# The end of an attention and gated-FFN kernel: the last unit's value blocks in one PSUM bank, its heads in one operand, the last chunks shared evenly

## The chip, the core and the metric

The kernel runs on one core of a Trainium2 chip. Its engines run side by side, each in its own instruction order: PE (matrix products; PEld is its weight loading), DVE (vector operations), ACT (activations), POOL (general elementwise work), and SP, which here issues all transfers. Products are written to PSUM, eight banks of 128 partitions by 512 float32; the other memory on the core is SBUF. The metric is the device time of one execution in microseconds (us), lower is better.

## What is computed

```
xn  = layernorm(x)                          # x: 2048 x 512
q, k, v = split(xn @ wqkv), 32 heads of 16
o   = softmax(q k^T / 4) v                  # per head, 2048 x 2048 scores
s   = o @ wo                                # 512 x 512
y   = silu(((xn @ wg) * (xn @ wu)) @ wd)    # 1792 hidden columns
out = x + s * y
```

All is float32. Products of the projections and the FFN are split into hi and lo parts (a number rounded to the PE's fast float32 form, and the rest), and take three terms: hi x hi, hi x lo, lo x hi.

## The kernel before

**Units and blocks.** Attention runs over 32 units: a group of four heads times a chunk of 512 query rows, the chunk being the inner index. Unit 31 is thus the last group on the last chunk. A unit has 16 rounds, one for each 128 keys. A round has four positions, one for each head: a product `t` of keys and queries (L632) and its exponential on ACT (L634), and, until these run out, a score product and its maximum on DVE for a later unit. The main loop's block covers two rounds, eight positions, and then calls `values`, which issues `block` (L645): 16 products of exponentials with value columns, written to the four 32-partition quarters of one bank, `pv`. Each quarter holds a head's 16 output rows and a row with the sum of exponentials, in 32 rows. Positions run four ahead of the values.

**Banks.** Three banks have the tag "st", in turn for `t` and `pv`; three have the tag "s", for score products; two have the tag "misc", for the filler. A new tile waits until the one that held its bank before has been read.

**What becomes of pv.** The first block of a unit is copied to a sum in SBUF by ACT. Later ones are copied by ACT to `part` and added by POOL, or, in the last 21 rounds (`now[0] > NU * NT - LEAD // 4`), added straight from the bank by DVE (L653). When a unit is complete, `finish` transposes the sum on DVE in 32x32 blocks, divides by the sums of exponentials, transposes back, and stores the heads in the memory tensor `OD` of its chunk.

**The filler.** The `t` and `pv` products are interleaved with other PE work that a generator hands out, so many steps after each position: the projections, the FFN, and last `ending`. Most of this work comes as `pair`: two output tiles, each the sum of products with 64 contraction rows, one on the lower and one on the upper half of the array at a time. A pair has two halves of n steps; between them ACT reads one element of a bank (`look`, L294). `Filler.cycles` says over how many blocks a pair is spread, and `spread` shares the steps of a block out between its positions.

**The ending.** For each of the four chunks of 512 rows, o @ wo is made in two pairs of row tiles, z (L286, L290), 24 steps a pair. Chunks 0, 1 and 2 use complete heads: `o_split` loads the heads back from `OD` and splits them into hi and lo (`split_rows`, on POOL); `prepare` calls it as soon as a chunk's last unit is stored and buffers are there, and `until` lets a chunk begin three rounds behind that. `end` multiplies z by the stored silu(y) on DVE (L477), adds x on POOL, and stores the rows. Chunk 3 is split: `open_pair` makes the sum over heads 0 to 27, leaves the banks open, and the last four heads are added by `final`. Order of the pairs: chunk 0 (two), chunk 1 (two), the first open pair, chunk 2 (two), the second open pair. Their spread over blocks is the list `parts`, which `Filler.cycles` returns: 3 means three blocks, 2 two, 1 one.

**The tail.** The second half of the last open pair runs behind the last `pv`. Meanwhile `last_heads` takes unit 31's sum, in two halves of 256 columns: add the last pv (L692), transpose (L693), reciprocal, multiply (L695), transpose back (L696), then hi on ACT (L697) and lo on POOL. `final` multiplies each tile's columns with `wrh` and `wrl`, the hi and lo of the last four heads' rows of wo, laid at 16 of each 32 partitions, the others zero: hi x wrh, hi x wrl, lo x wrh (L554). Then `end` for the four last tiles, tile 1 all on DVE (L472, L473), tile 3 in two halves, tiles 0 and 2 with their add on POOL, and the stores.

PE, ACT, DVE and POOL keep the program's order; the order of SP's transfers is the scheduler's.

Of the kernel before, what the change touches and what calls it, by code (L numbers as in the profile page):

```python
# [11 lines left out]
F32 = mybir.dt.float32  # L12
F32R = mybir.dt.float32r
AF = mybir.ActivationFunctionType
OP = mybir.AluOpType
# [4 lines left out]
P = 128  # L20
S, D, H, DH, FF = 2048, 512, 32, 16, 1792
NT = S // P
NC = S // 512
# [8 lines left out]
LEAD = 86  # L32
# [16 lines left out]
def body(ctx, tc, x, wqkv, wo, wg, wu, wd, out):  # L49
    nc = tc.nc  # L50
# [3 lines left out]
    class Tied:  # L54

        on = True
# [14 lines left out]
    pool, sync = Tied(nc.gpsimd), Tied(nc.sync)  # L71
# [4 lines left out]
    def dmar(dst, src):  # L76
        sync.dma_start(dst.bitcast(F32), src.bitcast(F32))

    dram = ctx.enter_context(tc.tile_pool(name="dram", bufs=1, space=DRAM))
    keep = ctx.enter_context(tc.tile_pool(name="keep", bufs=1))  # L80
# [29 lines left out]
    fst = {}  # L110
# [6 lines left out]
    def psum(tag, name):  # L117
        ps, bufs = fst["ps"]
        return ps.tile([P, 512], F32, tag=tag, name=name, bufs=bufs[tag])
# [3 lines left out]
    def soon(n, fn):  # L123

        if n:
            waiting.append((steps[0] + n, fn))
            waiting.sort(key=lambda w: w[0])
        else:
            fn()
# [10 lines left out]
    before_values, behind_values = [], []  # L140
# [93 lines left out]
            return nc.vector.tensor_scalar(xt, xt, e[:, t:t + 1], mr[:, t:t + 1], op0=OP.mult, op1=OP.add)  # L234
        return nc.scalar.activation(xt, xt, AF.Identity, bias=mr[:, t:t + 1], scale=e[:, t:t + 1])

    def split_rows(raw, hi, lo):
        pool.tensor_copy(hi, raw)
        pool.tensor_tensor(lo, raw, hi, op=OP.subtract)

    def ln_turn(tt):
        c, t = divmod(tt, 4)
# [196 lines left out]
    def o_split(c, tiles):  # L439

        for d, (oh, ol) in enumerate(tiles):
            heads = 8 if c < NC - 1 or d < ND - 1 else 4
            n = heads * DH
            raw = (wtile(("w1r", "w0r")[d]).rearrange("p d q -> p (d q)") if d < 2 else
                   fst["fp"].tile([P, D], F32, name="wdr", bufs=2))
            dma(raw[:n], OD[c][8 * d:8 * d + heads, 0:DH])
            soon(4 + 5 * d // 2, lambda raw=raw[:n], oh=oh[:n], ol=ol[:n]: split_rows(raw, oh, ol))
        ops[c] = now[0], tiles

    def small_tiles():  # L450
# [15 lines left out]

    def end(c, t, o, yt, xt):
        tt = 4 * c + t
        if t % 2 and c == NC - 1:
            for h in range(1 if t == 1 else 2):  # L470
                part = slice(None) if t == 1 else slice(256 * h, 256 * h + 256)
                nc.vector.tensor_tensor(o[:, part], o[:, part], yt[:, part], op=OP.mult)  # L472
                nc.vector.tensor_tensor(yt[:, part], o[:, part], xt[:, part], op=OP.add)  # L473
                dma(out[tt * P:(tt + 1) * P, part], yt[:, part])
            return
        else:
            nc.vector.tensor_tensor(yt, o, yt, op=OP.mult)  # L477
            if c < NC - 1:
                behind_values.append(lambda: add(tt, yt, xt))
                return  # L480
            pool.tensor_tensor(yt, yt, xt, op=OP.add)
        dma(out[tt * P:(tt + 1) * P], yt)

    def add(tt, yt, xt):
        pool.tensor_tensor(yt, yt, xt, op=OP.add)
        dma(out[tt * P:(tt + 1) * P], yt)

    def o_terms(c, t):
# [5 lines left out]
    def ending():  # L494


        fp = fst["fp"]

        def big(n):
            return fp.tile([P, 5, 512], F32R, name=n)  # L500

        side = [big(n).bitcast(F32) for n in ("hh", "dl")]
        fst["big", 1] = big("hl"), big("dh")

        def until(c):
            while c not in ops or now[0] < ops[c][0] + SPLIT_ROUNDS:
                yield

        def chunk(c):
            yield from until(c)  # L510
            for t in range(0, 4, 2):
                here = side[t // 2]
                got = [(here[:, n], here[:, 2 + n]) for n in range(2)]

                def loads(t=t, here=here):
                    dma(here[:, 0:2], YD[c][:, t:t + 2])
                    dma(here[:, 2:4], x[(4 * c + t) * P:(4 * c + t + 2) * P].rearrange("(t p) d -> p t d", p=P))
                soon(2, loads)
                outs = []
                yield from pair(outs, [("misc", f"z{c}_{u}") for u in (t, t + 1)], [o_terms(c, u) for u in (t, t + 1)])  # L520
                for n, o in enumerate(outs):
                    before_values.append(lambda u=t + n, o=o, got=got[n]: end(c, u, o, *got))

        banks = []

        def open_pair(t, tag):
            outs = []
            ts = [o_terms(NC - 1, u) for u in (t, t + 1)]
            yield from pair(outs, [(tag, f"z{NC - 1}_{u}") for u in (t, t + 1)],
                            [a[:-3] for a in ts], [a[-3:] for a in ts], stop=False)  # L530
            banks.extend(outs)

        yield from chunk(0)
        fst["first"] = True
        yield from chunk(1)
        fst["big", 2] = big("hl"), big("dh")
        wr = fp.tile([P, D], F32, name="e2", bufs=1)
        pool.memset(wr, 0.0)
        for j in range(4):
            dma(wr[32 * j:32 * j + DH], wo[(H - 4 + j) * DH:(H - 3 + j) * DH])  # L540
        wrh, wrl = [t[:, 4] for t in fst["big", 2]]
        pool.tensor_copy(wrh, wr)
        pool.tensor_tensor(wrl, wr, wrh, op=OP.subtract)
        yield from until(NC - 1)
        yield from open_pair(0, "s")
        yield from chunk(2)
        xr = side[0][:, :4]
        dma(xr, x[(NC - 1) * 512:].rearrange("(t p) d -> p t d", p=P))

        def final(todo, kinds):  # L550
            for n in kinds:
                k, r = ((0, wrh), (0, wrl), (1, wrh))[n]
                for t in todo:
                    nc.tensor.matmul(banks[t], fst["t"][k][:, t * P:(t + 1) * P], r, start=False, stop=n == 2,  # L554
                                     skip_group_check=True)
            if 2 in kinds:
                for t in todo:
                    end(NC - 1, t, banks[t], fst["y"][:, t], xr[:, t])

        yield from open_pair(2, "misc")  # L560
        while "t" not in fst:
            yield
        for todo in (0, 1), (2, 3):
            final(todo, (0, 1))
            final(todo, (2,))

    NU = NG * NC
    QS, MX = {}, {}
    sums = {}
# [67 lines left out]
    def block(todo):  # L637

        i = todo[0][0]
        g = i // NC  # L640
        o = psum("st", f"pv{i}")
        for n, (_, kt, es) in enumerate(todo):
            for j in range(4):
                h0 = (4 * g + j) * VW
                nc.tensor.matmul(o[32 * j:32 * j + 32], V[:, kt, h0:h0 + 32], es[j],  # L645
                                 start=n == 0, stop=n == len(todo) - 1)
        if todo[-1][1] == NT - 1 and i == NU - 1:
            last_heads(o)
        elif todo[0][1] == 0:
            sums[i] = keep.tile([P, 512], F32, name="acc", bufs=2)  # L650
            nc.scalar.activation(sums[i], o, AF.Copy)
        elif now[0] > NU * NT - LEAD // 4:
            nc.vector.tensor_tensor(sums[i], o, sums[i], op=OP.add)  # L653
        else:
            part = part_tile()
            nc.scalar.activation(part, o, AF.Copy)  # L656
            pool.tensor_tensor(sums[i], sums[i], part, op=OP.add)
# [23 lines left out]

    def last_heads(o):

        i = NU - 1
        acc = sums.pop(i)
        tr = keep.tile([P, 16, 32], F32, name="tr", bufs=1)
        rc = keep.tile([P, 16, 1], F32, name="rc", bufs=1)
        th, tl = fst["t"] = [fst["fp"].tile([P, 512], F32, name="g", bufs=2).bitcast(F32R) for _ in range(2)]
        for h in range(2):
            c, b = slice(256 * h, 256 * h + 256), slice(8 * h, 8 * h + 8)  # L690
            flat = tr[:, b].rearrange("p b e -> p (b e)")
            nc.vector.tensor_tensor(acc[:, c], o[:, c], acc[:, c], op=OP.add)  # L692
            nc.vector.transpose(flat, acc[:, c])  # L693
            nc.vector.reciprocal(rc[:, b], tr[:, b, DH:DH + 1])
            nc.vector.tensor_tensor(tr[:, b, 0:DH], tr[:, b, 0:DH], rc[:, b].to_broadcast([P, 8, DH]), op=OP.mult)  # L695
            nc.vector.transpose(acc[:, c], flat)  # L696
            nc.scalar.activation(th[:, c], acc[:, c], AF.Copy)  # L697
            pool.tensor_tensor(tl[:, c], acc[:, c], th[:, c], op=OP.subtract)


    def run(gen):
# [130 lines left out]
    now = [0]  # L832
# [107 lines left out]
    with tc.manual_schedule(engines=ORDERED):  # L940
# [4 lines left out]
        q = 0  # L945
        for b in range(NU * NT // 2):
            if fil.done:
                parts = iter([3, 2, 3, 2, 2, 2, 1, 2])
                fil = Filler(ending(), lambda n: next(parts))
            work = fil.begin()  # L950
            if b >= NU * NT // 2 - 2:
# [50 lines left out]
```

## Time and profile before

| | us |
|---|---|
| median of 3 runs | 1711.33 (1711.22 to 1714.48) |
| the profiled execution | 1711.65 |
| its span in the trace | 1709.9 |
| mean granted PE clock of the span | 0.999 |
| last score maxima on DVE | about 1628 us into the span |
| last pv starts | 1695.76 us into the span |

Times in the trace are in us from the start of the span. "1663.49 1.92 PE L645 MATMUL pv<-e,V ... x16" is a group of 16 products that began at 1663.49 and ended 1.92 later; in brackets stands how long the engine was idle before, and what released it. In a row of stretches the first number is the length, then follow for each engine its busy time and, in brackets, its instructions, the granted clock, the share of the transfer engines, and GB/s.

### The profile page before, as it was taken

The page shows a single profiled execution, that of the slowest core. Times are in us where ns is not written, and L with a number is a line of the kernel's source. Part 1 is how long each engine was busy: PE and PEld are TensorE (multiplying, and loading weights), DVE is VectorE, ACT ScalarE, POOL GpSimd, SP SyncE. Part 2 cuts the span into 40 slices and gives each one's busy share as a digit, 9 for nine tenths or more (in the row PEclk, how much of TensorE's full clock was granted, in tenths as well). Part 3 has the DMA queues.
Part 4 walks back from the last instruction along what each step waited for, and adds up shares of the span by engine and source line. Part 5 has one row for each costly group of instructions (what it writes and reads, how often), then busy time and mean ns, then how long its engine had stood idle before and what let it go on. Part 6 is the DMA issues. An engine that isn't in the chain of part 4 may idle for free. (4 is left out here: it accounts for less than half of the span.)

```text
span 1709.9 us, 35015 instructions
## 1 busy us (share of the span) xinstructions
PE 1700.0 (99%) x13574; PEld 1043.2 (61%) x13574; DVE 1430.8 (84%) x2479; ACT 1308.5 (77%) x2568; POOL 888.2 (52%) x889
## 2 busy tenths in 40 slices
PE   9999999999999999999999999999999999999998
PEld 6666656666666666656656666666666666666655
DVE  6888888888888888888888888888888888888933
ACT  6357877777777778778877887877778787777774
POOL 5315545762644647446354672663637546346672
PEclk9999999999999999999999999999999999999999
DMA  5317623620241312412115220320225112011352
GB/s 209 108 48 215 242 105 126 152 66 20 63 91 36 103 57 67 90 48 61 30 53 133 71 70 21 94 70 27 62 83 121 54 36 73 27 54 48 124 177 78
DMA packets 117378, 145.79 MB, mean 85 GB/s; under 512 B 12636, under 2 KB 74332, under 8 KB 114524
## 3 DMA queue, kind: packets, MB, share of 16 engines
q1 hardware_dynamic: 117212, 143.55, 28.8%
q8 instruction: 107, 1.75, 0.4%
q14 instruction: 59, 0.48, 0.1%
HBM read 95.94 MB, written 47.45 MB: 84 GB/s over the span
## 5 line engine op out<-in xcount | busy, mean ns | idle before, releaser
L612 DVE TENSOR_REDUCE mx<-s 128x1 f32<-128x512 f32 x2048 | 1255.6, 683 | 210.5 <-PE s L610 172.6
L634 ACT ACTIVATE e<-t 128x512 f32<-128x512 f32 x2048 | 1100.9, 601 | 97.7 <-PE pv L645 46.6
L632 PE MATMUL t<-qs,ks 50*128 50x512 f32 x2048 | 781.9, 408 | 0.0
L610 PE MATMUL s<-ks,qs 48*128 48x512 f32 x2048 | 767.0, 409 | 0.2
L63 POOL TENSOR_TENSOR acc<-acc,part 128x512 f32<-128x512 f32 x214 | 279.8, 1308 | 582.5 <-ACT part L656 582.0
L632 PEld LDWEIGHTS t<-qs,ks 50*128 50x128 f32 x2048 | 359.2, 185 | 271.0 <-issue 110.2
L645 PE MATMUL pv<-e,V 128*32 128x512 f32 x4096 | 492.5, 598 | 0.0
L610 PEld LDWEIGHTS s<-ks,qs 48*128 48x128 f32 x2048 | 350.8, 185 | 26.5 <-issue 3.6
L656 ACT ACTIVATE part<-pv 128x512 f32<-128x512 f32 x214 | 128.1, 599 | 204.9 <-PE pv L645 204.9
L645 PEld LDWEIGHTS pv<-e,V 128*32 128x32 f32 x4096 | 107.0, 109 | 242.0 <-issue 216.8
L290 PE MATMUL g<-fh,w1h 64*128 64x512 f32 x224 | 90.5, 404 | 0.0
L286 PE MATMUL u<-fh,w0h 64*128 64x512 f32 x224 | 90.4, 404 | 0.0
L290 PE MATMUL y<-dh,hh 64*128 64x512 f32 x224 | 89.6, 400 | 0.0
L286 PE MATMUL y<-dh,hh 64*128 64x512 f32 x224 | 88.8, 397 | 0.0
L290 PE MATMUL u<-fh,w0l 64*128 64x512 f32 x224 | 88.2, 394 | 0.0
L290 PE MATMUL g<-fl,w1h 64*128 64x512 f32 x224 | 88.0, 393 | 0.0
L286 PE MATMUL g<-fl,w1h 64*128 64x512 f32 x224 | 88.0, 393 | 0.0
L286 PE MATMUL u<-fh,w0l 64*128 64x512 f32 x224 | 88.0, 393 | 0.0
L290 PE MATMUL g<-fh,w1l 64*128 64x512 f32 x224 | 88.0, 393 | 0.0
L286 PE MATMUL g<-fh,w1h 64*128 64x512 f32 x224 | 87.9, 392 | 0.0
L290 PE MATMUL u<-fl,w0h 64*128 64x512 f32 x224 | 87.8, 392 | 0.0
L286 PE MATMUL y<-dl,hh 64*128 64x512 f32 x224 | 87.8, 392 | 0.0
(262 smaller groups left out, 2982.5 us busy)
## 6 DMA issues: line engine op xcount, KB each, us to landing
w1r<-in_wg_dram SPq DMA_DIRECT2D x56, 256.0 KB
w0r<-in_wu_dram SPq DMA_DIRECT2D x56, 256.0 KB
wdr<-in_wd_dram SPq DMA_DIRECT2D x56, 256.0 KB
qs<-QD SPq DMA_DIRECT2D x64, 192.0 KB
ks<-KD SPq DMA_DIRECT2D x12, 768.0 KB
KD<-hl SPq DMA_DIRECT2D x16, 512.0 KB
QD<-hl SPq DMA_DIRECT2D x16, 512.0 KB
OD<-acc SPq DMA_DIRECT2D x31, 256.0 KB
```

The lines of the kernel that those rows point to most:

```text
L63: got = getattr(self.engine, name)(*args, **kw)
L286: nc.tensor.matmul(outs[k], l[LOWER], r[LOWER], start=k == 0 and n == 0, stop=(stop or k == 0) and n == len(low) - 1, skip_group_check=k == 1)
L290: nc.tensor.matmul(outs[1 - k], l[UPPER], r[UPPER], start=k == 0 and m == 0, stop=(stop or k == 0) and m == len(high) - 1, skip_group_chec ...
L610: nc.tensor.matmul(o, QS[i][b:b + KB, pr, t * P:(t + 1) * P], k[b:b + KB, pr, kc * 512:(kc + 1) * 512], start=True, stop=True)
L612: nc.vector.tensor_reduce(MX[i][:, j, t, kc:kc + 1], o, axis=AX.X, op=OP.max)
L632: nc.tensor.matmul(o, k[b:b + KR, pr, kt * P:(kt + 1) * P], QS[i][b:b + KR, pr], start=True, stop=True)
L634: nc.scalar.activation(e, o, AF.Exp, scale=DH ** -0.5)
L645: nc.tensor.matmul(o[32 * j:32 * j + 32], V[:, kt, h0:h0 + 32], es[j], start=n == 0, stop=n == len(todo) - 1)
L656: nc.scalar.activation(part, o, AF.Copy)
```

## The change

Unit 31's blocks all go to one bank, from the "s" tag, as a single sum over its 16 rounds; the copy and the adds of its `pv` are gone. In `last_heads` DVE transposes that bank straight, POOL makes hi and lo of the divided heads beside each other in the 32 columns of a block (`both`), DVE transposes both back at once, and ACT rounds the result. `wrh` is copied to the other 16 of each 32 partitions by four small transfers, so that one product gives (hi + lo) x wrh and a second hi x wrl. `final` runs tile by tile. In the last 21 rounds every second split of `o_split` and the residual adds of `add` go to DVE. At the end tile 1's add goes to POOL and tile 2's to DVE. The list `parts` is 3, 2, 2, 2, 2, 2, 2, 2 instead of 3, 2, 3, 2, 2, 2, 1, 2.

```diff
-    def split_rows(raw, hi, lo):
-        pool.tensor_copy(hi, raw)
-        pool.tensor_tensor(lo, raw, hi, op=OP.subtract)
+    def split_rows(raw, hi, lo, on=None):
+        on = on or pool
+        on.tensor_copy(hi, raw)
+        on.tensor_tensor(lo, raw, hi, op=OP.subtract)
+
+    def late():
+        return now[0] > NU * NT - LEAD // 4
...
-            soon(4 + 5 * d // 2, lambda raw=raw[:n], oh=oh[:n], ol=ol[:n]: split_rows(raw, oh, ol))
+            soon(4 + 5 * d // 2, lambda d=d, raw=raw[:n], oh=oh[:n], ol=ol[:n]:
+                 split_rows(raw, oh, ol, nc.vector if late() and d % 2 else pool))
...
-        if t % 2 and c == NC - 1:
-            for h in range(1 if t == 1 else 2):
-                part = slice(None) if t == 1 else slice(256 * h, 256 * h + 256)
+        if t == 3 and c == NC - 1:
+            for h in range(2):
+                part = slice(256 * h, 256 * h + 256)
...
+        (nc.vector if t == 2 else pool).tensor_tensor(yt, yt, xt, op=OP.add)
         dma(out[tt * P:(tt + 1) * P], yt)
...
     def add(tt, yt, xt):
-        pool.tensor_tensor(yt, yt, xt, op=OP.add)
+        (nc.vector if late() else pool).tensor_tensor(yt, yt, xt, op=OP.add)
...
+        for j in range(0, P, 32):
+            dmar(wrh[j + DH:j + 32], wrh[j:j + DH])
...
-        def final(todo, kinds):
-            for n in kinds:
-                k, r = ((0, wrh), (0, wrl), (1, wrh))[n]
-                for t in todo:
-                    nc.tensor.matmul(banks[t], fst["t"][k][:, t * P:(t + 1) * P], r, start=False, stop=n == 2,
-                                     skip_group_check=True)
...
+        def final(t):
+            for n, r in enumerate((wrh, wrl)):
+                nc.tensor.matmul(banks[t], fst["t"][:, t * P:(t + 1) * P], r, start=False, stop=n == 1,
+                                 skip_group_check=True)
...
-        o = psum("st", f"pv{i}")
+        whole = i == NU - 1
+        if whole and todo[0][1] == 0:
+            fst["last"] = psum("s", "last")
+        o = fst["last"] if whole else psum("st", f"pv{i}")
...
-                                 start=n == 0, stop=n == len(todo) - 1)
+                                 start=(kt if whole else n) == 0, stop=kt == NT - 1 if whole else n == len(todo) - 1,
+                                 skip_group_check=whole)
...
-        th, tl = fst["t"] = [fst["fp"].tile([P, 512], F32, name="g", bufs=2).bitcast(F32R) for _ in range(2)]
+        both, fst["t"] = [fst["fp"].tile([P, 512], F32, name="g", bufs=2).bitcast(F32R) for _ in range(2)]
+        back = keep.tile([P, 512], F32, name="acc", bufs=2)
+        both = both.rearrange("p (b e) -> p b e", e=32)
+        flat = "p b e -> p (b e)"
         for h in range(2):
             c, b = slice(256 * h, 256 * h + 256), slice(8 * h, 8 * h + 8)
...
-            nc.vector.tensor_tensor(acc[:, c], o[:, c], acc[:, c], op=OP.add)
-            nc.vector.transpose(flat, acc[:, c])
+            nc.vector.transpose(tr[:, b].rearrange(flat), o[:, c])
             nc.vector.reciprocal(rc[:, b], tr[:, b, DH:DH + 1])
             nc.vector.tensor_tensor(tr[:, b, 0:DH], tr[:, b, 0:DH], rc[:, b].to_broadcast([P, 8, DH]), op=OP.mult)
-            nc.vector.transpose(acc[:, c], flat)
-            nc.scalar.activation(th[:, c], acc[:, c], AF.Copy)
-            pool.tensor_tensor(tl[:, c], acc[:, c], th[:, c], op=OP.subtract)
+            pool.tensor_copy(both[:, b, 0:DH], tr[:, b, 0:DH])
+            pool.tensor_tensor(both[:, b, DH:32], tr[:, b, 0:DH], both[:, b, 0:DH], op=OP.subtract)
+        for h in range(2):
+            c, b = slice(256 * h, 256 * h + 256), slice(8 * h, 8 * h + 8)
+            nc.vector.transpose(back[:, c], both[:, b].rearrange(flat).bitcast(F32))
+            nc.scalar.activation(fst["t"][:, c], back[:, c], AF.Copy)
...
-                parts = iter([3, 2, 3, 2, 2, 2, 1, 2])
+                parts = iter([3, 2, 2, 2, 2, 2, 2, 2])
```

More of the change, by code (lines that the diff above doesn't have):

```diff
@@ L475, in end @@
             return
[L476 to L480, printed above, removed]
-            pool.tensor_tensor(yt, yt, xt, op=OP.add)
+        nc.vector.tensor_tensor(yt, o, yt, op=OP.mult)
+        if c < NC - 1:
+            behind_values.append(lambda: add(tt, yt, xt))
+            return
+        (nc.vector if t == 2 else pool).tensor_tensor(yt, yt, xt, op=OP.add)
         dma(out[tt * P:(tt + 1) * P], yt)
     def add(tt, yt, xt):
-        pool.tensor_tensor(yt, yt, xt, op=OP.add)
+        (nc.vector if late() else pool).tensor_tensor(yt, yt, xt, op=OP.add)
         dma(out[tt * P:(tt + 1) * P], yt)
@@ L548, in ending @@
         dma(xr, x[(NC - 1) * 512:].rearrange("(t p) d -> p t d", p=P))
-        def final(todo, kinds):
-            for n in kinds:
-                k, r = ((0, wrh), (0, wrl), (1, wrh))[n]
-                for t in todo:
-                    nc.tensor.matmul(banks[t], fst["t"][k][:, t * P:(t + 1) * P], r, start=False, stop=n == 2,
-                                     skip_group_check=True)
-            if 2 in kinds:
-                for t in todo:
-                    end(NC - 1, t, banks[t], fst["y"][:, t], xr[:, t])
+        def final(t):
+            for n, r in enumerate((wrh, wrl)):
+                nc.tensor.matmul(banks[t], fst["t"][:, t * P:(t + 1) * P], r, start=False, stop=n == 1,
+                                 skip_group_check=True)
         yield from open_pair(2, "misc")
@@ L562, in ending @@
             yield
-        for todo in (0, 1), (2, 3):
-            final(todo, (0, 1))
-            final(todo, (2,))
+        for t in range(4):
+            final(t)
+        for t in range(4):
+            end(NC - 1, t, banks[t], fst["y"][:, t], xr[:, t])
     NU = NG * NC
@@ L645, in block @@
                 nc.tensor.matmul(o[32 * j:32 * j + 32], V[:, kt, h0:h0 + 32], es[j],
-                                 start=n == 0, stop=n == len(todo) - 1)
-        if todo[-1][1] == NT - 1 and i == NU - 1:
-            last_heads(o)
+                                 start=(kt if whole else n) == 0, stop=kt == NT - 1 if whole else n == len(todo) - 1,
+                                 skip_group_check=whole)
+        if whole:
+            if todo[-1][1] == NT - 1:
+                last_heads(o)
         elif todo[0][1] == 0:
@@ L651, in block @@
             nc.scalar.activation(sums[i], o, AF.Copy)
-        elif now[0] > NU * NT - LEAD // 4:
+        elif late():
             nc.vector.tensor_tensor(sums[i], o, sums[i], op=OP.add)
@@ L682, in last_heads @@
     def last_heads(o):
-        i = NU - 1
-        acc = sums.pop(i)
         tr = keep.tile([P, 16, 32], F32, name="tr", bufs=1)
         rc = keep.tile([P, 16, 1], F32, name="rc", bufs=1)
-        th, tl = fst["t"] = [fst["fp"].tile([P, 512], F32, name="g", bufs=2).bitcast(F32R) for _ in range(2)]
+        both, fst["t"] = [fst["fp"].tile([P, 512], F32, name="g", bufs=2).bitcast(F32R) for _ in range(2)]
+        back = keep.tile([P, 512], F32, name="acc", bufs=2)
+        both = both.rearrange("p (b e) -> p b e", e=32)
+        flat = "p b e -> p (b e)"
         for h in range(2):
             c, b = slice(256 * h, 256 * h + 256), slice(8 * h, 8 * h + 8)
-            flat = tr[:, b].rearrange("p b e -> p (b e)")
-            nc.vector.tensor_tensor(acc[:, c], o[:, c], acc[:, c], op=OP.add)
-            nc.vector.transpose(flat, acc[:, c])
+            nc.vector.transpose(tr[:, b].rearrange(flat), o[:, c])
             nc.vector.reciprocal(rc[:, b], tr[:, b, DH:DH + 1])
             nc.vector.tensor_tensor(tr[:, b, 0:DH], tr[:, b, 0:DH], rc[:, b].to_broadcast([P, 8, DH]), op=OP.mult)
-            nc.vector.transpose(acc[:, c], flat)
-            nc.scalar.activation(th[:, c], acc[:, c], AF.Copy)
-            pool.tensor_tensor(tl[:, c], acc[:, c], th[:, c], op=OP.subtract)
+            pool.tensor_copy(both[:, b, 0:DH], tr[:, b, 0:DH])
[4 more added lines that the diff above has]
+            nc.scalar.activation(fst["t"][:, c], back[:, c], AF.Copy)
     def run(gen):
```

## The prediction

> **What bounds the kernel now.** I read the page's engine totals first, then the stretches between the value products of the last twelve blocks, then the timeline of one such block, and last the timeline of the tail.
>
> ```profile
> span 1709.9 us, 35015 instructions
> PE 1700.0 (99%) x13574; PEld 1043.2 (61%) x13574; DVE 1430.8 (84%) x2479; ACT 1308.5 (77%) x2568; POOL 888.2 (52%) x889
> ...
> core 0: us, PE busy (x) PEld busy (x) DVE busy (x) ACT busy (x) POOL busy (x), PEclk, DMA share, GB/s
> 1628.91:1634.55 5.64, 5.64 (x42) 2.73 (x40) 1.94 (x6) 4.66 (x10) 4.54 (x5) 1.00 0.29 99
> 1634.55:1640.12 5.57, 5.48 (x39) 2.50 (x39) 0.69 (x1) 4.73 (x11) 5.33 (x7) 1.00 0.65 213
> 1640.12:1645.61 5.49, 5.49 (x42) 3.18 (x43) 0.80 (x2) 4.13 (x9) 4.82 (x5) 1.00 0.58 180
> 1645.61:1651.58 5.97, 5.97 (x50) 3.31 (x49) 3.98 (x7) 4.56 (x9) 2.99 (x3) 1.00 0.42 147
> 1675.42:1681.38 5.96, 5.96 (x50) 3.37 (x48) 0.69 (x1) 4.39 (x10) 0.00 (x0) 1.00 0.00 0
> 1681.38:1690.47 9.09, 9.07 (x74) 5.84 (x73) 2.05 (x4) 4.83 (x10) 2.53 (x2) 1.00 0.34 115
> 1690.47:1695.76 5.29, 5.29 (x42) 2.99 (x41) 1.91 (x3) 2.28 (x4) 2.54 (x2) 1.00 0.53 201
> ```
>
> The change touches nothing ahead of about 1629 us, so only the last 81 us count. A stretch runs from the start of one block's value products (pv) to the next; it holds 8 expo products t and the filler's z steps, each step a lower and an upper half-array product side by side. Old filler shares for the first pair of the second chunk are 8, 7 and 9 steps: the first three rows, 16.70 us. The second pair of the third chunk has all 24 steps in one block, 9.09 us. Every other block has 12 steps and takes 5.96 or 5.97. POOL and DVE are far from full here; ACT is under 85% of each. What sets a 12-step block is the PE queue:
>
> ```profile
> 1663.49 1.92 PE L645 MATMUL pv<-e,V 128*32 128x512 f32 x16
> 1664.58 0.60 ACT L634 ACTIVATE e<-t 128x512 f32<-128x512 f32 x1 [0.81 <-PE pv L645]
> 1665.35 0.50 PE L632 MATMUL t<-qs,ks 50*128 50x512 f32 x2
> 1665.48 0.69 DVE L653 TENSOR_TENSOR acc<-pv,acc 128x512 f32<-128x512 f32 x1 [5.27 <-PE pv L645]
> 1665.88 3.82 ACT L634 ACTIVATE e<-t 128x512 f32<-128x512 f32 x7 [0.70 <-PE t L632]
> 1665.92 0.39 PE L286 MATMUL z<-fl,w0h 64*128 64x512 f32 x1
> 1666.23 0.18 PEld L632 LDWEIGHTS t<-qs,ks 50*128 50x128 f32 x1 [0.36 <-DVE acc L653]
> 1666.57 0.39 PE L286 MATMUL z<-fh,w0l 64*128 64x512 f32 x1
> 1666.81 0.39 PE L286 MATMUL z<-fh,w1h 64*128 64x512 f32 x1
> 1669.13 0.39 PE L286 MATMUL z<-fh,w0l 64*128 64x512 f32 x1
> 1669.45 0.16 PEld L645 LDWEIGHTS pv<-e,V 128*32 128x32 f32 x8 [0.36 <-ACT e L634]
> ```
>
> Products on one half of the array follow each other every 0.23 to 0.24 us (1666.57 to 1666.81). The third t takes the bank that pv held, and stands until DVE has added pv into its sum (1665.48 + 0.69). From 1665.92 the next lower product was due at 1666.15; t went at 1666.23, and the one behind it came 0.34 later, 0.11 over the pitch. The wait costs 0.08 + 0.11, about 0.18 us a block, not the 0.36 that its row shows for the weight loader.
>
> A light block has a second limit. With 8 steps, four fewer, PE alone would need 5.96 - 4 x 0.233 = 5.03; the rows show 5.5 to 5.6. Three banks hold the t, so the eighth waits for the fifth exponential. From pv's start that loop is 1665.88 - 1663.49 = 2.39 to the first exponential, five at 3.82/7 = 0.546, and 1669.45 - 1669.13 = 0.32 into pv: 5.44, beside rows of 5.49 to 5.64.
>
> **The change, part by part.** *The shares* (3,2,3,2,2,2,1,2 become 3,2,2,2,2,2,2,2). The sum stays 17 blocks, so the last pair still ends behind the last pv; from the second chunk on each pair comes one block earlier, at 12 steps a block. The gates do not stop that: the third chunk's rows are asked for at the second chunk's end plus one position, in round 499, and the gate opens in round 502, when the products before it end in round 502; the margin before is the same. The double block also pays once for the read that closes a pair's first half, elsewhere hidden under pv:
>
> ```profile
> 1686.59 0.40 PE L632 MATMUL t<-qs,ks 50*128 50x512 f32 x1
> 1687.01 0.18 PEld L286 LDWEIGHTS z<-fh,hl 64*128 64x128 f32 x1 [0.46 <-ACT look L294]
> ```
>
> Three light blocks and the double one, 16.70 + 9.09 = 25.79, become four of 12. I take 6.00 for the first, where ACT still copies pv out (0.03 over the next), and 5.97 for three: 23.91. That is **-1.88**. Not all of it is the look wait (0.42 + 0.11): the rest is the light blocks' idle PE, which now carries work.
>
> *One bank for the last unit's value blocks.* The ACT copy and six DVE adds go, and no pv takes a t bank in the last unit. The "s" pool has three banks and nobody scores any more; the open pair takes two, this the third, so nothing waits. Replacing the four blocks above left six of 12 steps behind the last unit's pv: the old 5.90, 6.01, 5.96, 5.97, 5.96 for the blocks from 1651.58 to 1681.38 and one of my four. Without the stall I take 5.96 - 0.18 = 5.78 each. New sum from 1628.91 to 1695.76: 6.00 + 3 x 5.97 + 6 x 5.78 + 5.29 = 63.88 beside 66.85, so shares and bank together give **-2.97**, -1.88 and -1.09. Bounds: no gain by the bank, where the fourth t waits for the first exponential instead (it ends 1.13 us after the first t starts, and the fourth t is due at 1.05 to 1.27): 6 x 5.96, -1.89 in all. The other end is ACT's loop, 5.49: -4.7. I keep 5.78, since in half of the blocks the fourth t is due after that exponential.
>
> *Splits and residual adds to DVE.* Four splits and four adds leave POOL (0.61 and 1.29 each by the row below) for DVE, idle over 3 us of each of these blocks. Cost nothing: their rows are loaded several us ahead, and behind them DVE has only the bank-freeing multiplies, blocks later. Without that cover each costs about 0.7 on DVE (the 128x512 add of 1665.48).
>
> *Copies of wrh.* Four small transfers on SP, after POOL's cast and subtract, which wait for the second chunk's last product:
>
> ```profile
> 1657.42 0.61 POOL L63 CAST hl<-e 128x512 fp32r<-128x512 f32 x1 [8.16 <-PE z L290]
> 1658.11 1.28 POOL L63 TENSOR_TENSOR dh<-e,hl 128x512 fp32r<-128x512 f32 x1
> 1651.08 2.00 SPq L63 DMA_DIRECT2D e<-in_wo_dram  x1
> ```
>
> They come six us earlier now and are used 45 us later: nothing, unless SP stands behind them (a rival).
>
> *The tail.* Now two halves run one after the other, each DVE add, transpose, reciprocal, multiply, transpose, then ACT's hi, then POOL's lo; six products per pair of tiles.
>
> ```profile
> 1697.81 0.42 DVE L692 TENSOR_TENSOR acc<-pv,acc 128x256 f32<-128x256 f32 x1 [4.65 <-PE pv L645]
> 1698.27 0.45 DVE L693 STREAM_TRANSPOSE tr<-acc 128x256 f32<-128x256 f32 x1
> 1698.98 0.29 DVE L695 TENSOR_TENSOR tr<-tr,rc 128x128 f32<-128x128 f32 x1
> 1699.31 0.45 DVE L696 STREAM_TRANSPOSE acc<-tr 128x256 f32<-128x256 f32 x1
> 1699.79 0.42 ACT L697 ACTIVATE g<-acc 128x256 fp32r<-128x256 f32 x1 [3.21 <-DVE acc L696]
> 1700.29 0.73 POOL L63 TENSOR_TENSOR g<-acc,g 128x256 fp32r<-128x256 f32 x1 [6.58 <-ACT g L697]
> 1700.82 0.35 DVE L695 TENSOR_TENSOR tr<-tr,rc 128x128 f32<-128x128 f32 x1
> 1702.02 0.69 DVE L477 TENSOR_TENSOR y<-z,y 128x512 f32<-128x512 f32 x1 [0.38 <-PE z L554]
> 1702.86 1.29 POOL L63 TENSOR_TENSOR y<-y,hh 128x512 f32<-128x512 f32 x1
> 1704.18 3.21 SPq L63 DMA_DIRECT2D out_dram<-y  x5
> 1704.78 1.27 POOL L63 TENSOR_TENSOR y<-y,hh 128x512 f32<-128x512 f32 x1 [0.62 <-DVE y L477]
> 1706.00 0.42 DVE L473 TENSOR_TENSOR y<-z,hh 128x256 f32<-128x256 f32 x1
> ```
>
> New, on the old clock from 1697.81: transpose to multiply takes 1699.31 - 1698.27 = 1.04 a half, so both are done at 1699.90. POOL's cast and subtract of 128 columns are not in the trace; between an 8-column operation at 0.20 and the 256-column subtract at 0.73 I take 0.30 and 0.46, with 0.08 between: the first half's rows stand at 1699.75, the second's at 1700.80. DVE turns back the first at 1699.92 to 1700.37, ACT rounds it until 1700.82, PE starts at about 1700.87 and needs two products for the first tile instead of three: its end at 1701.11 + 0.39. DVE's first multiply goes at **1701.54** instead of 1702.02, -0.48. Behind it DVE has the same eight operations (4.40 to 1706.42): the third tile's add came to DVE, the second's went to POOL. The last POOL add now ends about 3.4 behind the first multiply, 1704.95 instead of 1706.05, so SP's five issues no longer queue behind it: the last ends at about 1706.6 instead of 1707.39. Tail **-0.7**; bounds 0.3 worse (POOL at its 256- and 512-column times, 0.73 and 0.61) and -1.2.
>
> ```profile
> L63 POOL TENSOR_TENSOR e<-e,mr 128x8 f32<-128x8 f32 x1 | 0.2, 203 | 0.1
> ```
>
> DVE's second multiply took 0.35 while POOL subtracted (1700.29 to 1701.02), and 0.29 with POOL idle: 0.06 more. The Trainium skill (SBUF — State Buffer, Who interferes with whom) says that a DVE instruction with two SBUF inputs and a GpSimd instruction that reads SBUF lock each other out for a whole instruction. By that rule the multiply here would have been held from 1700.82 to 1701.02, 0.20; the trace shows a third of that. In the new tail the second half's multiply falls into POOL's work on the first: the sum would be 0.2 less by the rule, 0.06 less by the row.
>
> **Sum.** -2.97 - 0.7 = -3.67 on the profiled execution's 1711.65 (span 1709.9 and 1.75 around it): 1707.98. That execution stands 0.32 above the median 1711.33, so I forecast **1707.7**, 0.21% less. What a measurement can tell from no change is about 0.2%, 3.4 us, and the forecast stands just beyond it.
>
> **Rivals.**
>
> *The bank frees nothing.* t4 waits for the first exponential in every block and blocks stay at 5.96. For it: the wait and the exponential are 0.1 apart. Against: the fourth t is due later in half of the blocks. 1711.33 - 1.89 - 0.7 = 1708.7.
>
> *The tail gives nothing.* POOL now stands between DVE's two transposes; at its longer bound the second half's rows come late and DVE waits in front of both the turn back and the first multiply. For it: POOL's 256-column subtract is 0.73 against DVE's 0.42. Against: the first half's POOL work is covered by DVE's second half. 1711.33 - 2.97 + 0.3 = 1708.7; with the rival above, 1709.7.
>
> *Third chunk's rows late: slower.* SP issues in order. The second chunk's products end just ahead of a pv at 1628.91 + 6.00 + 3 x 5.97 = 1652.8, so POOL's subtract ends at about 1655, and the wrh copies issue from there; at 2.00 each, the longest of the small loads, they hold SP to 1663. The third chunk's products start at 1652.8 + 2 x 5.78 + 1.86 (pv to t, 1663.49 to 1665.35), 1666.2, and row loads and splits behind the copies end past that. Each us that they are late stops PE, exponentials too, since t and z share its queue. It decides when the first product comes later than 1669.9 (1666.2 and the 3.67 to be lost); at 4 to 6 us, 1712 to 1714. For it: the loads have moved six us nearer to their use. Against: the first rows' load issued well ahead of its products, and a short transfer took 0.3 to 0.6.
>
> *The shares do not move.* A gate missed by a round leaves a block without z, and 12 steps (2.8 us) fall behind the last pv, ahead of the tail: 1711.33 - 3.67 + 2.8, 1710.5. The round count above speaks against it.
>
> **How the numbers follow.** Forecast 50%, bank frees nothing 18%, tail gives nothing 14%, gate missed 5%, late rows 6%; 7% for blocks that fall toward ACT's loop, 1706.0 to 1707. The range 1706.0 to 1710.8 holds all but the late rows and a part of the missed gate, with room for the run-to-run spread. Of the forecast's 50 I put 43 below 1707.9 (its own range is 1707.0 to 1708.3) and 7 above, with 2 of the two partial rivals below: faster 43 + 7 + 2 = 52%, slower 7%, within 0.2% the rest, 41%.
>
> **What would show it.** Right: 12 steps in each of the last blocks, no block near 9 us, stretches near 5.78 behind the last unit's pv without a wait of t for pv's bank, the first multiply of the tail some 3.8 us behind its first transpose, and POOL's last add ahead of DVE's end. Wrong: t4 waiting for ACT in 5.96 us blocks; POOL operations of 0.6 in the tail with DVE idle in front of the turn back; PE idle ahead of the third chunk's first products. Equal times with all these in place would mean that the light blocks' idle PE was not idle.

## The result, and the profile after

The changed kernel takes 1710.29 us in the median of 14 runs (1707.99 to 1711.97), the one before 1713.07 beside it (14 runs, 1710.98 to 1714.63). The ratio is 0.9984, 95% interval 0.9977 to 0.9991: 0.16% faster, some 2.8 us. The profiled execution took 1709.33, its span 1706.5.

The stretches of the changed kernel from one block's value products to the next, columns as before. The last two rows are the whole from the same pv to the last pv, first the changed kernel, then the one before:

```profile
core 0: us, PE busy (x) PEld busy (x) DVE busy (x) ACT busy (x) POOL busy (x), PEclk, DMA share, GB/s
1628.60:1634.53 5.93, 5.93 (x50) 3.46 (x48) 2.94 (x8) 4.95 (x10) 4.74 (x5) 1.00 0.22 75
1634.53:1640.57 6.04, 6.04 (x50) 3.37 (x48) 2.00 (x3) 4.97 (x11) 5.79 (x7) 1.00 0.66 203
1640.57:1646.54 5.97, 5.97 (x50) 3.31 (x49) 3.18 (x5) 4.36 (x9) 1.61 (x2) 1.00 0.51 149
1652.49:1658.28 5.79, 5.79 (x47) 3.52 (x45) 5.58 (x6) 4.23 (x9) 5.55 (x6) 1.00 0.50 138
1681.43:1687.22 5.79, 5.79 (x50) 3.53 (x48) 0.00 (x0) 4.25 (x10) 0.00 (x0) 1.00 0.59 184
1687.22:1692.50 5.28, 5.28 (x43) 2.99 (x41) 2.49 (x4) 2.51 (x5) 0.00 (x0) 1.00 0.27 99
1628.60:1692.50 63.90, 63.90 (x517) 37.96 (x515) 22.78 (x37) 46.64 (x92) 19.05 (x18) 1.00 0.44 139
1628.91:1695.76 66.85, 66.74 (x517) 38.06 (x515) 15.43 (x27) 47.48 (x93) 34.52 (x34) 1.00 0.41 133
```

The light blocks and the double block are gone, every block is near 6, and behind the last unit's first pv near 5.8. The whole is 63.90 instead of 66.85: 2.95 us, where the sum said 2.97. (The trace starts this part 0.31 earlier than the one before, 1628.60 against 1628.91; that lies in the part that the change does not touch.)

The tail of the changed kernel, from its timeline:

```profile
1694.57 0.45 DVE L699 STREAM_TRANSPOSE tr<-last 128x256 f32<-128x256 f32 x1 [4.76 <-PE last L650]
1695.65 0.29 POOL L63 CAST g<-tr 128x128 fp32r<-128x128 f32 x1 [36.04 <-DVE tr L701]
1696.02 0.47 POOL L63 TENSOR_TENSOR g<-tr,g 128x128 fp32r<-128x128 f32 x1
1696.22 0.42 DVE L701 TENSOR_TENSOR tr<-tr,rc 128x128 f32<-128x128 f32 x1
1696.56 0.43 DVE L706 STREAM_TRANSPOSE acc<-g 128x256 f32<-128x256 f32 x1
1697.02 0.42 ACT L707 ACTIVATE g<-acc 128x256 fp32r<-128x256 f32 x1 [3.77 <-DVE acc L706]
1697.49 0.19 PEld L558 LDWEIGHTS z<-hl,g 128*128 128x128 f32 x1 [0.55 <-ACT g L707]
1698.27 1.89 DVE L481 TENSOR_TENSOR y<-z,y 128x512 f32<-128x512 f32 x3 [0.26 <-PE z L558]
1699.04 1.28 POOL L63 TENSOR_TENSOR y<-y,hh 128x512 f32<-128x512 f32 x1 [1.51 <-DVE y L481]
1700.19 0.69 DVE L485 TENSOR_TENSOR y<-y,hh 128x512 f32<-128x512 f32 x1
1700.28 1.73 POOL L63 TENSOR_TENSOR y<-y,hh 128x512 f32<-128x512 f32 x1
1700.35 3.48 SPq L63 DMA_DIRECT2D out_dram<-y  x5
1702.19 0.42 DVE L478 TENSOR_TENSOR y<-z,hh 128x256 f32<-128x256 f32 x1
```

DVE's first multiply comes 5.77 behind the start of the last pv (1692.50), 6.26 before (1702.02 - 1695.76): 0.49 earlier, as the sum had it. DVE's end follows, 10.11 instead of 10.66. But the span ends 14.00 behind the last pv instead of 14.14. Of 0.7 only 0.14 arrived, and the place is in the last rows: POOL's second add took 1.73, not the 1.27 of before, while DVE added tile 2 (1700.19 to 1700.88). Tile 1's store waited for it until 1702.01, and behind it in SP's queue stood tile 2's rows, ready since 1700.88, and the first half of tile 3's, ready since 1701.68.

Together 2.95 + 0.14 = 3.09 us, 0.18%.

### The profile page after: what moved, and what is told of

The parts are those of the page before. It is cut to its first block, busy times and chain, and to the rows that moved or that the text cites. A ratio compares the mean times of both kernels' runs of the same rounds, so it can differ in the third digit from the quotient of the medians.

```text
span 1706.5 us, 34991 instructions
## 1 busy us (share of the span) xinstructions
PE 1695.8 (99%) x13570; PEld 1043.1 (61%) x13570; DVE 1436.8 (84%) x2487; ACT 1307.8 (77%) x2567; POOL 872.6 (51%) x875
## 3 DMA queue, kind: packets, MB, share of 16 engines
q8 instruction: 106, 1.74, 0.4%
## 4 chain that ended last, share of the span: by engine, by line
PE 97%; DVE 1%; ACT 1%; issue 0%; POOL 0%; DMA 0%; ACTq 0%
PE pv L650 27%; PE t L634 19%; PE s L612 12%; PE g L290 6%; PE y L290 5%; PE u L290 5%; PE g L294 5%; PE y L294 4%; PE u L294 4%; PE p L290 3%; PE v L271 2%; PE p L294 2%; PE z L290 2%; PE z L294 1%; PE last L650 1%; PE p L271 1%
## 5 line engine op out<-in xcount | busy, mean ns | idle before, releaser
L650 PE MATMUL pv<-e,V 128*32 128x512 f32 x3968 | 477.1, 598 | 0.0
L294 PE MATMUL g<-fh,w1l 64*128 64x512 f32 x224 | 88.0, 393 | 0.0
L290 PE MATMUL g<-fh,w1l 64*128 64x512 f32 x224 | 87.8, 392 | 0.0
```

Of the source, the lines that this page charges most:

```text
L290: nc.tensor.matmul(outs[k], l[LOWER], r[LOWER], start=k == 0 and n == 0, stop=(stop or k == 0) and n == len(low) - 1, skip_group_check=k == 1)
L294: nc.tensor.matmul(outs[1 - k], l[UPPER], r[UPPER], start=k == 0 and m == 0, stop=(stop or k == 0) and m == len(high) - 1, skip_group_chec ...
```

## The experiments

Each ran beside the kernel before on the same chip. A microsecond is 0.06% here, about a third of the width of an interval of such a ratio; sizes are therefore read from the trace, one execution each, and the ratios say only whether they agree. Where two kernels share such a part, their traces agree within 0.03 (stretch 66.85 and 66.83, tail 14.14 and 14.11 or 14.00 and 14.03); the four kernels with the changed stretch gave 63.86 to 63.98. "Stretch" is from the pv at 1628.91 (and its like) to the last pv, "tail" from there to the end of the span.

### The shares alone

```diff
-                parts = iter([3, 2, 3, 2, 2, 2, 1, 2])
+                parts = iter([3, 2, 2, 2, 2, 2, 2, 2])
```

> The kernel before with the new list of shares (3,2,2,2,2,2,2,2) and nothing else. My theory: the stretch from the pv at 1628.91 to the last pv (66.85 us before) shrinks by 1.9, to about 64.95: three light blocks and the double one (25.79) become four blocks of 6.00 and 5.97, and every block still has the third t waiting for pv's bank. Time 0.11% less than before. Rival, the light blocks' idle PE was not free: the four blocks keep about 25.8 in sum, stretch 66.8, time the same. The tail behind the last pv stays as it was (14.1 us to the span's end).

The first three blocks, the one in the place of the old double block, and the whole stretch:

```profile
1631.86:1637.79 5.93, 5.93 (x50) 3.46 (x48) 1.94 (x6) 4.95 (x10) 4.74 (x5) 1.00 0.22 73
1637.79:1643.82 6.03, 6.03 (x51) 3.30 (x49) 0.69 (x1) 4.98 (x11) 5.79 (x7) 1.00 0.66 212
1643.82:1649.79 5.97, 5.97 (x50) 3.53 (x48) 1.98 (x3) 4.35 (x9) 5.81 (x7) 1.00 0.60 172
1685.55:1691.51 5.96, 5.96 (x50) 3.32 (x48) 0.69 (x1) 4.41 (x10) 0.00 (x0) 1.00 0.53 176
1631.86:1696.79 64.93, 64.93 (x517) 36.92 (x515) 15.42 (x27) 47.80 (x93) 34.43 (x34) 1.00 0.43 135
```

66.85 to 64.93, the tail 14.11: the shares are worth 1.92 us. Ratio 0.9988 (0.9979 to 0.9996). PE executes the same products; what it gains is idle time, which the page's 99% busy does not show. By the 0.233 a step of the prediction the three light blocks would take 3 x 5.97 - 12 x 0.233 = 15.1 instead of 16.70, and the double one 5.97 + 12 x 0.233 = 8.8 instead of 9.09: an estimate of 1.6 in the light blocks and 0.3 in the double one, where the prediction put 0.42 + 0.11 on the look.

### What sets a light block

```diff
-                parts = iter([3, 2, 3, 2, 2, 2, 1, 2])
+                parts = iter([3, 2, 5, 2, 2, 1, 1, 1])
```

> The kernel before with the second chunk's first pair spread over five blocks (5, 5, 4, 5, 5 steps) instead of three (8, 7, 9), and the double blocks that follow from it later. Theory, the loop through ACT and the three banks sets a light block: these five last about 5.4 to 5.6 us, as long as those with 8 steps. Rival, PE's work sets them: 5.96 less 7 x 0.233, about 4.3.

Five light blocks, and the first of 12 steps behind them, from a single execution. Only these are read: the pairs behind them are packed otherwise, and the end of this variant does not compute the kernel's output. The last two lines are waits at the end of the third light block.

```profile
1630.52:1636.16 5.64, 5.54 (x36) 2.26 (x34) 1.94 (x6) 4.66 (x10) 4.45 (x5) 1.00 0.22 68
1636.16:1641.68 5.52, 5.31 (x35) 2.21 (x35) 0.69 (x1) 4.67 (x10) 5.28 (x7) 1.00 0.57 187
1641.68:1647.20 5.52, 5.37 (x33) 2.19 (x32) 0.69 (x1) 4.17 (x10) 4.86 (x5) 1.00 0.73 212
1647.20:1652.68 5.48, 5.33 (x34) 2.26 (x34) 2.79 (x5) 4.13 (x9) 0.00 (x0) 1.00 0.12 36
1652.68:1658.26 5.58, 5.53 (x35) 2.26 (x34) 0.71 (x2) 4.63 (x10) 0.00 (x0) 1.00 0.29 97
1658.26:1664.29 6.03, 6.03 (x50) 3.31 (x49) 1.27 (x2) 4.60 (x9) 2.98 (x3) 1.00 0.36 114
...
1646.70 0.18 PEld L632 LDWEIGHTS t<-qs,ks 50*128 50x128 f32 x1 [0.31 <-ACT e L634]
1647.20 0.16 PEld L645 LDWEIGHTS pv<-e,V 128*32 128x32 f32 x8 [0.32 <-ACT e L634]
```

Four or five steps take 5.48 to 5.64, as eight did. A block has a floor at about 5.5 that PE's work does not set. The loop through ACT and three banks (5.44) has it there, and the last t and the next pv of the block wait for an exponential. That it is this loop and no other is argued from these waits; no run has a fourth bank.

### The bank alone

```diff
-        o = psum("st", f"pv{i}")
+        whole = i == NU - 1
+        if whole and todo[0][1] == 0:
+            fst["last"] = psum("s", "last")
+        o = fst["last"] if whole else psum("st", f"pv{i}")
...
-            nc.vector.tensor_tensor(acc[:, c], o[:, c], acc[:, c], op=OP.add)
-            nc.vector.transpose(flat, acc[:, c])
+            nc.vector.transpose(flat, o[:, c])
```

> The kernel before with the last unit's value blocks summed in one bank of the score pool, and last_heads reading that bank; shares, hi and lo operands, splits and adds as before. My theory: the blocks behind the last unit's first pv lose 0.11 once (ACT copy) and 0.18 in four blocks, the double block and the last one nothing: stretch 66.85 to about 66.0, with no wait of t for pv's bank left. Rival, the fourth t takes the wait over: blocks stay at 5.96 and the stretch at 66.85. In the tail the two DVE adds are gone, so the first multiply comes about 0.4 earlier behind the last pv (from 6.26 to about 5.85 behind the start of the last pv).

A block of the last unit, the whole stretch, and four lines of the tail, beside one of the kernel before:

```profile
1654.53:1660.31 5.78, 5.78 (x50) 3.72 (x48) 0.00 (x0) 4.27 (x10) 0.05 (x1) 1.00 0.53 163
1631.87:1697.84 65.97, 65.86 (x517) 38.65 (x515) 11.27 (x21) 46.37 (x92) 34.47 (x34) 1.00 0.41 133
```

```profile
1701.93 0.73 POOL L63 TENSOR_TENSOR g<-acc,g 128x256 fp32r<-128x256 f32 x1 [6.16 <-ACT g L701]
1702.01 0.80 DVE L699 TENSOR_TENSOR tr<-tr,rc 128x128 f32<-128x128 f32 x1
1702.63 0.30 PEld L554 LDWEIGHTS z<-hl,g 128*128 128x128 f32 x2 [0.35 <-issue]
1704.10 0.69 DVE L477 TENSOR_TENSOR y<-z,y 128x512 f32<-128x512 f32 x1 [0.81 <-PE z L554]
```

```profile
1700.55 0.30 PEld L554 LDWEIGHTS z<-hl,g 128*128 128x128 f32 x2 [0.35 <-ACT g L697]
```

The stretch fell by 0.88 to 65.97, as expected; no t waits for pv's bank in the last unit, and the fourth t does not take the wait over. The tail did not gain the 0.4 that was expected: the first multiply stands 6.26 behind the last pv's start (1697.84), exactly as before, and the span's end 14.16. PE holds it. The first half's rounded heads stand at 1701.86, 4.02 behind the last pv's start (4.45 before: 1699.79 + 0.42 - 1695.76), but `final` begins 4.79 behind it in both (1702.63 and 1700.55), straight after the z steps that PE still has to issue, and the multiply follows 1.47 later in both. The second half's division took 0.80, 0.29 without POOL's subtract of the first half beside it; the first multiply does not wait for that. Ratio 0.9995 (0.9986 to 1.0004).

### The new tail without the bank

The changed kernel with the old shares, the old bank and all splits and residual adds on POOL; DVE adds the last pv to the sum first:

```diff
+            nc.vector.tensor_tensor(back[:, c], o[:, c], back[:, c], op=OP.add)
-            nc.vector.transpose(tr[:, b].rearrange(flat), o[:, c])
+            nc.vector.transpose(tr[:, b].rearrange(flat), back[:, c])
```

> The new tail (both operands in one, two products a tile, tile 1's add on POOL, tile 2's on DVE) on the old shares and the old bank, so DVE still adds the last pv to the sum, 0.42 for each half; splits and residual adds on POOL as before. Stretch ahead of the last pv as before, 66.85. If the tail's gain came from the new operand, the first multiply would come earlier than 6.26 behind the start of the last pv; I expect it later, at about 6.5, because both halves' adds and divisions (2.92) now run ahead of the first turn back, and the gain of the changed kernel came from the missing adds. To the span's end 14.1 to 14.6.

```profile
1695.38 0.16 PEld L647 LDWEIGHTS pv<-e,V 128*32 128x32 f32 x8 [0.36 <-issue]
1701.13 0.19 PEld L558 LDWEIGHTS z<-hl,g 128*128 128x128 f32 x1 [1.31 <-ACT g L703]
1701.91 1.89 DVE L481 TENSOR_TENSOR y<-z,y 128x512 f32<-128x512 f32 x3 [0.27 <-PE z L558]
```

The stretch is 66.83 and the first multiply 6.53 behind the last pv's start (1701.91 - 1695.38), the tail 14.72: 0.6 worse, just over the expected 14.6. Ratio 1.0003 (0.9994 to 1.0012). So neither half of the tail's change gains alone, 14.16 and 14.72 against 14.14. The time from the last pv's start to the first weight load of `final`, and from there to DVE's first multiply, says why:

| | start of `final` | to the first multiply | sum |
|---|---|---|---|
| before, and the bank alone | 4.79 | 1.47 | 6.26 |
| the new tail without the bank | 5.75 | 0.78 | 6.53 |
| the changed kernel | 4.99 | 0.78 | 5.77 |

The old order makes five products before the first tile is complete, the new one two. With the adds still there two halves of 1.4 run ahead of the first turn back, and PE waits for ACT until 5.75; without them its operand lets it start at 4.99, only 0.20 later than the z steps do. So the missing adds gain only together with the shorter `final`.

### Tile 2's add with one SBUF input

```diff
-        if t == 3 and c == NC - 1:
-            for h in range(2):
-                part = slice(256 * h, 256 * h + 256)
+        if t > 1 and c == NC - 1:
+            for h in range(t - 1):
+                part = slice(None) if t == 2 else slice(256 * h, 256 * h + 256)
...
-        (nc.vector if t == 2 else pool).tensor_tensor(yt, yt, xt, op=OP.add)
+        pool.tensor_tensor(yt, yt, xt, op=OP.add)
```

> The changed kernel, but tile 2's product is left in its PSUM bank and its add reads the bank and x, as tile 1's did before: DVE's add has one SBUF input instead of two. Theory A, the shared port: POOL's second add in the tail, 1.73 in the changed kernel where DVE's add with two SBUF inputs ran, goes back to 1.27 to 1.30, the last four stores are issued about 0.45 earlier behind the first multiply, and the end of the span comes 0.3 to 0.5 earlier behind the last pv (14.0 in the changed kernel). Theory B, POOL is slow for another reason (its two adds back to back): it stays at about 1.7 and the end stays. The stretches ahead of the last pv stay at 63.9.

```profile
1700.66 2.50 POOL L63 TENSOR_TENSOR y<-y,hh 128x512 f32<-128x512 f32 x2 [1.50 <-DVE y L481]
1701.10 0.69 DVE L477 TENSOR_TENSOR z<-z,y 128x512 f32<-128x512 f32 x1
1701.82 0.69 DVE L478 TENSOR_TENSOR y<-z,hh 128x512 f32<-128x512 f32 x1
1701.97 3.02 SPq L63 DMA_DIRECT2D out_dram<-y  x5
```

POOL's two adds take 2.50 together, 2.96 in the changed kernel, though DVE works beside them as much as there. The span's end comes 13.57 behind the last pv, 0.43 earlier, and the stretch is 63.87. DVE's second input from SBUF is the cause, as theory A has it; two adds back to back are not. Ratio to the kernel before 0.9983 (0.9975 to 0.9992).

### Two queues for the last stores

The same kernel, and the stores of tiles 0 and 1 issued by ACT:

```diff
         pool.tensor_tensor(yt, yt, xt, op=OP.add)
-        dma(out[tt * P:(tt + 1) * P], yt)
+        nc.scalar.dma_start(out[tt * P:(tt + 1) * P], yt)
```

> The changed kernel with tile 2's add from its bank, and with the stores of tiles 0 and 1 (those that wait for POOL) issued by ACT, the others by SP. Theory: what is left of the tail's missing gain is SP's order: tile 2's store and the two halves of tile 3 stand behind tile 1's, and 768 KB then go at some 350 GB/s in one bunch. With two queues each store goes when its rows stand; span's end 0.3 to 0.5 earlier behind the last pv, about 13.1 to 13.3 after 13.57. Rival: the transfers' latency sets the end, not the queue, since the last half's rows stand only 0.3 ahead of its issue; then 13.4 to 13.6. Stretches ahead of the last pv 63.9.

```profile
1702.66 1.56 ACTq L486 DMA_DIRECT2D out_dram<-y  x2
```

```profile
1703.22 2.06 SPq L63 DMA_DIRECT2D out_dram<-y  x3
1704.95 0.33 SPq L63 DMA_DIRECT2D out_dram<-y  x1
```

The last store is issued 0.04 behind the rows that it carries (DVE's end at 1704.91) and the tail falls to 13.08, 0.49 less again; the stretch is 63.98. With both edits the tail gives 1.06 us over the one before. The kernel has the lowest median, 1708.64, and the lowest ratio, 0.9973 (0.9962 to 0.9983), though the interval still overlaps that of the changed kernel.

### Splits and adds back on POOL

```diff
-                 split_rows(raw, oh, ol, nc.vector if late() and d % 2 else pool))
+                 split_rows(raw, oh, ol, pool))
...
-        (nc.vector if late() else pool).tensor_tensor(yt, yt, xt, op=OP.add)
+        pool.tensor_tensor(yt, yt, xt, op=OP.add)
```

> The changed kernel with all splits and residual adds back on POOL. In the changed kernel POOL's two splits of the third chunk end at 1659.6 and DVE's at 1661.7, and its first products start at about 1666. All four and two more adds on POOL take 4 x 1.9 + 2.5 from 1654.4 and end at about 1664.6. My theory: still in time, stretch from the pv before the last FFN-free blocks to the last pv as in the changed kernel (63.9), time the same; the splits' move to DVE is worth nothing. Rival: the rows come late now that the chunk begins a block earlier, and the block of the third chunk's first pair grows by 0.5 to 3 us over 5.79: then the move is what makes the earlier start possible.

POOL's last split, the block that uses it, and the stretch:

```profile
1665.07 1.28 POOL L63 TENSOR_TENSOR dh<-wdr,hl 128x512 fp32r<-128x512 f32 x1
```

```profile
1665.77:1671.55 5.78, 5.78 (x50) 3.63 (x48) 0.00 (x0) 4.23 (x9) 0.58 (x1) 1.00 0.39 124
1630.31:1694.17 63.86, 63.86 (x517) 37.98 (x515) 11.27 (x21) 46.59 (x92) 34.45 (x34) 1.00 0.43 139
```

The move is worth nothing: 63.86 and a tail of 14.03, ratio 0.9981 (0.9972 to 0.9991). The last split ends 1.6 ahead of the third chunk's first product (1667.96), so POOL alone is in time.

## Why the prediction was right, and where its sizes were off

**The shares** were to give 1.88 and gave 1.92 alone. The step on which it hung, that a light block lasts about 5.5 whatever it holds, stood the test with four and five steps. Why it does, the loop through ACT, stays argued.

**The bank** was to give 1.09 with the shares, and by the expectation of its run about 0.85 without; alone it gave 0.88, with the shares 1.03 (64.93 to 63.90), and the blocks came to 5.78 to 5.80 where 5.78 was taken. Reading the wait as 0.08 of delay and 0.11 of a slower next product, and not as the loader's 0.36, was right: 0.36 would have given blocks of 5.6. The rival in which the fourth t takes over fell.

**Moves to DVE, and the wrh copies**, were taken at nothing; the moves are worth nothing either way. No run leaves the copies out. The rivals of late rows and of a missed gate did not come: the third chunk's products began at 1666.25, where the prediction had 1666.2, without a wait of PE.

**The tail** is the term that was mis-sized: 0.7 forecast, 0.14 measured. Its front was right (0.48 forecast, 0.49 measured; POOL's cast and subtract 0.29 and 0.47 where 0.30 and 0.46 were taken). The step that failed is "The last POOL add now ends about 3.4 behind the first multiply", and with it that SP's issues "no longer queue behind it": the add ended 3.74 behind, at 1702.01, and four of the five issues stood behind it. The sum moved an add with two SBUF inputs to DVE beside POOL's adds and gave both their undisturbed times, although the paragraph below it weighed just this lock for another pair. The last issue was to end 0.79 earlier and ended 0.30 earlier, 11.33 behind the last pv's start (1703.83) instead of 11.63. Of the difference the add makes 0.33 (3.74 against 3.41), and the four issues behind it 0.17 (1.82 against 1.65). The span's end then came 2.67 behind the last issue, 2.51 before. These 0.16 go with three 128-row tiles in one bunch behind 1702, where before two tiles had gone earlier; that the bytes cause it is argued, not tested. In size the tail came close to the rival in which it gives nothing, but not by that rival's mechanism: POOL's cast and subtract took nowhere near its 0.61 and 0.73, and the first multiply came as forecast. With the input and the queue mended it gave 1.06, more than was forecast.

**The lock** was also read wrongly. From 0.35 against 0.29 the prediction had the trace show "a third" of the rule. The rows agree with the rule in full: where POOL's subtract is at work when DVE's multiply starts, the multiply ends 0.15 behind POOL's end, whenever it was issued. Before, 1700.29 + 0.73 = 1701.02 and 1700.82 + 0.35 = 1701.17; with the bank alone 1702.66 and 1702.81; in the changed kernel 1696.49 and 1696.64. In the new tail without the bank both multiplies miss the subtracts and take 0.29. The extra time seen in one row, 0.06, was small because DVE came late in POOL's instruction; the same pair in another phase cost 0.51, more than the whole 0.29 of the multiply, which equal sharing would not give.

**The total**: 3.67 forecast, 3.09 in the traces, 2.8 in the medians. The forecast of 0.21% stood just beyond the 0.2% that the prediction took as the least that can be told from no change; the missing half microsecond of the tail put the result, 0.16%, below that, though its interval, 0.9977 to 0.9991, does not reach 1. That 1710.29 lies within 1706.0 to 1710.8 is in part the width of the range: the kernel before stood at 1713.07 beside it, 1.74 above the 1711.33 from which the forecast was taken, and from there the same sum gives 1709.4.

## What to carry to other kernels

In a pipelined loop with work woven in, look for blocks that last as long with less in them: something other than PE's work sets their floor, here by the waits a loop through buffers, and evening the shares turns PE's idle time there into work although PE shows 99% busy. Cost a bank wait by the pitch of the products around it, not by the loader's idle time. Before taking work off the way to an operand, ask when the engine that takes the operand is free. When an operation with two SBUF inputs moves to DVE, list what POOL reads at that moment, and at the very end of a kernel give each store a queue in which it does not stand behind rows that come later.

## What the runs showed of the hardware

A DVE multiply with two SBUF inputs that meets a POOL subtract does not share with it: it ends 0.15 behind POOL's end in three traces, 0.15 to 0.16 in the four others where the two meet, and lost from 0.06 to 0.51 by its phase. The other way round, POOL's add took 1.73 instead of 1.28 beside DVE's two-input add, and stayed at 1.25 a piece beside the same add with one input in PSUM. This is what the Trainium skill states (SBUF — State Buffer, Who interferes with whom: whoever comes first holds the shared port for its whole instruction), and these traces agree. A cast on DVE, which has one SBUF input, was slowed beside POOL too: it took 1.52 in the changed kernel at 1655.93 and 0.38 at 1630.65, and POOL's subtract beside it 1.63 instead of 1.28. No run takes this pair apart. In the middle of the kernel such meetings cost nothing: the block with this one (1652.49 to 1658.28) lasted 5.79, as the others did, and as it did with all splits on POOL.

```profile
1630.65 0.38 DVE L239 CAST w1h<-w0r 128x512 fp32r<-128x512 f32 x1
...
1655.54 1.63 POOL L63 TENSOR_TENSOR dh<-w1r,hl 128x512 fp32r<-128x512 f32 x1
1655.93 1.52 DVE L239 CAST hl<-w0r 128x512 fp32r<-128x512 f32 x1
```
